# Sums of weight blocks made early and kept in DRAM, and the first products of a two-piece part taken piece by piece

## The chip, the core and the metric

The kernel is one program on one core of a Trainium2 chip. The metric is the device time of one execution in microseconds (us). The core has five engines that each run their own list of instructions in order: TensorE (PE; its weight loads are shown apart as PEld), VectorE (DVE), ScalarE (ACT), GpSimd (POOL) and SyncE (SP, which here only issues DMA transfers). An instruction waits on semaphores for the work of other engines and for transfers; whatever stands behind it on its engine waits with it.

## The reference, cut to what matters

Three stages follow one another: windowed attention, a gated MLP behind an RMS norm, and a second MLP with a softmax-like gate and a layer norm.

```python
x = attention(q, k, v)                      # 4 x 8 heads x 576 x 64; window of 32, or dilated by 4; as rows: 2304 x 512
xn = x / sqrt(mean(x * x) + 1e-06) * rms_g  # 512 wide
g = xn @ w_gate                             # 512 x 1536
y = (g / (1 + exp(-g)) * (xn @ w_val)) @ w_out        # back to 512
h = y @ w_in                                # 512 x 1024
e = exp(h - max(h)); solu = h * e / sum(e)
out = layer_norm(solu) * g_ln @ w_out2      # 2304 x 512
```

## The kernel before, in words

Every fp32 product is taken as three products of split numbers: a tensor is split into a high half (`xh`, `uh`, the first index of `w`), rounded by ACT (L304), and the rest, its low half, subtracted by DVE or POOL (L313). The helper `mm3` issues high by high, high by low and low by high (L890, L891, L892).

The 2304 rows are cut into nine pieces of 256. Parts 0, 2, 3 and 4 are two pieces (512 rows), part 1 is one. The work goes through these stages, by the clock of the profiled run: attention of the first pieces (0 to 32 us); the first MLP on part 0, while its weights come from DRAM and are split (v0 to v2, 32 to 153 us); part 1 (v3, to 219 us); part 2, pieces 3 and 4 (v4, to 344 us); parts 3 and 4 jointly (to 462 us); the second products of those two and the second MLP's weights (to 540 us); the second MLP on all 18 row tiles (to the end). Attention of later pieces (`scores`, L619; softmax on DVE and ACT; `values`, L665) runs between the MLP's matmuls, a few steps ahead of need. Where a piece's attention is done, its rows are normed and split into `xh` and `xl`.

Weights: for each of the twelve blocks f of 128 columns, SP fetches `w_gate`, `w_val` and `w_out` raw (L342; `raw` has five places), ACT and DVE rework the words (L357, L362, L366), ACT rounds the high half, DVE or POOL subtracts the low one. The halves stay in SBUF. For use much later, ACT also issues a copy of the plain words of `w_gate` and `w_val` to DRAM: step `kept`, L392, tile `pw`, 24 transfers of 256 KB.

The joint stage multiplies two parts by a pair of weight blocks with seven block products instead of eight (`m1` to `m7`, L1177), for twelve groups q. Four of the factors are sums and differences of weight blocks. In each group, `sload` (SP, L1140) reads two plain blocks back from `pw` into `sc`, `scomb` (L1145; DVE for q below 3, POOL from 3 on) makes four sums of 128x256, `shigh` (ACT, L304, into `shl`) and `slow` (DVE, L313) split them. Then come the products, with ACT copying partial sums from bank to bank in between (`seed`, L1184). `m7` needs both the split sums and a `seed` that stands behind `shigh` on ACT.

The second MLP makes each pair of row tiles r by seven block products, `p1` to `p7` (L1499 to L1501), from weights that are fetched and split at 468 to 533 us; ACT or DVE copy partial sums between them (`u2`: `ha` to `he`). The four column sums (L1507: `c11`, `c22`, `c21`, `c12`, DVE) read the banks of those products. Then a pair is normed, transposed (`t`, PE), split into `lt` (ACT, then DVE, L313) and multiplied by the last weights (`o`, L1572 to L1574). `y` L1432 are sums of loaded `y` blocks, made by DVE or POOL.

The order of all this is not written out. Each step is handed to a planner (`Plan`) with what it needs, the tiles it takes, the engines that may run it with a cost for each, and a due time. The planner simulates the engines by these costs, takes whichever ready step can start first (among those close together the one due first), and so fixes the engine of each step and the order on each engine. A table of small shifts to due times (`NUDGE`) is the same in both kernels. PE's order from 342 us on is forced by a list, `line`. A change of any cost or due time can thus move instructions anywhere.

Of the kernel before, what the change touches and what calls it, by code (L numbers as in the profile page):

```python
# [256 lines left out]
def tile_attention_glu_solu(ctx: ExitStack, tc: tile.TileContext, qk_d, v_d, w1_d, win2_d, wout2_d,  # L257
# [71 lines left out]
    def prepare(stage, f, cuts, srcs, scales, dues, needs=(), lead=((1, 0), "joined", 0)):  # L329
# [67 lines left out]
        for n, c in enumerate(cuts):  # L397
            w, due = 512 * len(c), dues[c[0]]
            one, two, act, pool_ = 0.15 + w / 1920, 0.15 + w / 960, 0.2 + w / 1200, 0.25 + w / 500
            plan.add((key, "shifted", n), {"a": act}, shifted(c), [(key, "fetch", i) for i in c], due=due)  # L400
            plan.add((key, "parts", n), {"d": one}, parts(c), [(key, "fetch", i) for i in c], due=due)
            plan.add((key, "joined", n), {"d": two}, joined(c), [(key, "parts", n), (key, "shifted", n)] +
                     [lead] * (key != lead[0]) + [(key, "joined", 0)] * (n > 0),
                     takes=([("wf", wf)] if n == 0 else []) + ([("cl", st), ("ch", (st, 1))] if (key, "joined", n) == lead else []),
                     uses=[wf, st, (st, 1)], due=due)
            before = [(key, "joined", n)]
            for i in c:
                if scales[i] is not None:
# [485 lines left out]
    def mlp(v, due):  # L894
# [60 lines left out]

        ready = [[(x, k, t) for t in pieces for x in ("high", "low")] for k in range(2)]
        ys = [("y", p, k) for k in range(KD)]
        for f in fs:
            d = due + 10 * f
            for part, key, shift in ((0, "g", 0), (1, "vp", 3)):  # L960
                for i, ks in enumerate(((0, 1), (2, 3))):
# [4 lines left out]
                    if part == 0 and i == 0 and (f > fs[0] or v in (1, 2)):  # L966
                        before = [("vp", v, f - 1, 1) if f > fs[0] else ("vp", v - 1, HALVES - 1, 1)]
                    plan.add(name, {"t": cost}, into(part, f, (key, v, f), ks),
                             before + [made[1, f, part]] + (ready[i] if f == fs[0] and part == 0 else []),
# [42 lines left out]
    def joint():  # L1012
# [22 lines left out]
        for f in range(STASHED):  # L1035
# [17 lines left out]
            add(("stash", f), {"s": 1.35}, keep_, [made[1, f, 2], ("g", 4, f // 2, 0)], due=150)  # L1053
# [66 lines left out]
        def group_(q):  # L1120
            fp, X = divmod(q, 2)
            fs = (2 * fp, 2 * fp + 1)
            sc, shl, far = ("sc", q), ("shl", q), q > 1 and q % 2 == 0
            tag_of = {"A": "a", "E": "a", "D": "a", "B": "g", "C": "vp"} if q % 2 == 0 else \
# [14 lines left out]
            def load(e):  # L1139
                nc.sync.dma_start(out=scratch().rearrange("p a m -> p (a m)"), in_=plain_w[fp, X].rearrange("p i m -> p (i m)"))  # L1140

            def combos(e):
                t = scratch()
                for out_, a, b, op in ((3, 2, 3, ALU.add), (2, 0, 2, ALU.subtract), (0, 3, 0, ALU.subtract), (1, 1, 0, ALU.subtract)):
                    ENG[e].tensor_tensor(t[:, out_], t[:, a], t[:, b], op)  # L1145

            key_c = [("scl",)] * far
# [141 lines left out]
    def operands(j, needs_of):  # L1289
# [79 lines left out]
    def w_out2():  # L1369

        st = ("stage", 2)
        for g in range(2):
# [8 lines left out]
            for i in range(4):  # L1381
# [16 lines left out]
                plan.add((key, "fetch"), {"s": 1.35}, lambda e, rw=rw, k=k: nc.sync.dma_start(out=words(rw).rearrange("p n t -> p (n t)"),  # L1398
# [194 lines left out]
    def second_stage(stage_1, last):  # L1593
# [73 lines left out]
        def tile_steps(i):  # L1667
# [3 lines left out]
            for q in range(2):  # L1671
# [3 lines left out]
                    takes=[lt] if q == 0 else [], uses=[tp[1], lt[1]], due=due - 60 if r else 5800)  # L1675
                add(("lt", i, q, 1), {"d": 0.7}, lambda e, q=q: p_lt(i, q, 1, e), [("lt", i, q, 0)], uses=[tp[1], lt[1]], due=due - 60 if r else 5800)
# [163 lines left out]
```

## Time and profile before

| | |
|---|---|
| median of 3 runs | 740.66 us (739.85 to 741.54) |
| profiled execution | 737.58 us |
| its span, first to last instruction | 735.8 us |
| PE busy | 715.8 us, 97% |
| DVE, ACT, POOL busy | 66%, 50%, 21% |
| granted TensorE clock, mean | 0.995 |
| moved by DMA | 90.94 MB, 124 GB/s in the mean |

Durations are read from the profiled execution, which lies 3.08 us under the median; 1.78 us of its time lie outside the span. A granted clock of 1.00 is the upper of TensorE's two levels (2.4 GHz). At that level matmuls of 512 columns follow each other every 0.23 us, although the records last 0.39 us, since they overlap.

### The profile page before, as it was taken

Reading aid. Unit: us, or ns where it says so; the run is one execution under the profiler, and the core shown is the slowest. Engines: PE = TensorE matmul, PEld = TensorE weight load, DVE = VectorE, ACT = ScalarE, POOL = GpSimd, SP = SyncE. Lnnn points to the kernel's source line nnn. Section 1 sums busy time; section 2 is a strip of 40 time slices with the busy share of each in tenths; the row PEclk is TensorE's granted clock in tenths of the full one; section 3 lists DMA queues with packets and bytes.
Section 4 is the critical chain, followed back from the end, with each engine's and each line's share of the span. In section 5 each row is a group of like instructions: output and inputs, shape, how many; then the busy total and the mean of one; then the engine's idle time right before and its main releaser. Section 6 shows DMA issues by size and latency. Waiting matters only on the chain.

```text
span 735.8 us, 11918 instructions
## 1 busy us (share of the span) xinstructions
PE 715.8 (97%) x4565; PEld 599.1 (81%) x4565; DVE 485.4 (66%) x933; ACT 368.5 (50%) x810; POOL 155.2 (21%) x181
## 2 busy tenths in 40 slices
PE   7988999999999999999999999999999999999998
PEld 5876878899997788888788888888777888888887
DVE  4876998555556657559777676688767776655552
ACT  2874745444554446334555555264455555444341
POOL 0210035222212122020455110046043110101110
PEclk9999999999999999999999999999999999999999
DMA  9989433232347643102411103784132111000001
GB/s 329 401 313 397 169 123 127 77 138 82 114 137 247 230 145 119 39 21 68 141 57 58 58 0 104 234 292 147 54 115 73 57 44 58 29 15 29 30 29 44
DMA packets 42009, 90.94 MB, mean 124 GB/s; under 512 B 4192, under 2 KB 14432, under 8 KB 41952
## 3 DMA queue, kind: packets, MB, share of 16 engines
q1 hardware_dynamic: 38496, 83.89, 33.1%
q10 hardware_dynamic: 3456, 6.29, 2.3%
q8 instruction: 36, 0.59, 0.3%
q14 instruction: 21, 0.17, 0.1%
HBM read 69.72 MB, written 20.45 MB: 123 GB/s over the span
## 4 chain that ended last, share of the span: by engine, by line
PE 79%; DMA 7%; DVE 4%; POOL 3%; issue 3%; ACT 2%; SPq 1%; ACTq 0%; POOLq 0%; DVEq 0%
PE ca L1177 6%; PE o L1573 4%; PE o L1572 4%; PE o L1574 4%; PE y L890 4%; PE g L890 4%; PE y L892 4%; PE y L891 4%; PE g L891 4%; PE g L892 4%; PE vp L890 4%; PE vp L892 3%; PE vp L891 3%; PE pv L665 3%; DMA raw<-w 3%
## 5 line engine op out<-in xcount | busy, mean ns | idle before, releaser
L1572 PE MATMUL o<-w,lt 128*128 128x512 f32 (+1 forms) x152 | 58.9, 388 | 0.0
L1574 PE MATMUL o<-w,lt 128*128 128x512 f32 (+1 forms) x152 | 57.6, 379 | 0.0
L1573 PE MATMUL o<-w,lt 128*128 128x512 f32 (+1 forms) x152 | 57.5, 379 | 0.0
L313 POOL TENSOR_TENSOR w<-wf,w 128x512 fp32r<-128x512 f32 (+1 forms) x15 | 30.5, 2038 | 122.8 <-ACT w L304 122.8
L890 PE MATMUL y<-uh,w 128*128 128x512 f32 (+1 forms) x148 | 54.1, 366 | 0.0
L892 PE MATMUL y<-uh,w 128*128 128x512 f32 (+1 forms) x148 | 51.8, 350 | 0.0
L891 PE MATMUL y<-uh,w 128*128 128x512 f32 (+1 forms) x148 | 51.7, 349 | 0.0
L632 ACT ACTIVATE s<-s,nm 128x64 f32<-128x64 f32 x120 | 40.2, 338 | 20.6 <-DVE nm L627 18.0
L1145 POOL TENSOR_TENSOR sc<-sc 128x256 f32<-128x256 f32 x36 | 33.5, 931 | 68.5 <-DMA yT<-yo 32.9
L921 ACT ACTIVATE u<-g 128x512 f32<-128x512 f32 (+1 forms) x37 | 19.1, 516 | 54.3 <-PE g L892 54.3
L772 POOL TENSOR_TENSOR sq<-x 128x256 f32<-128x256 f32 x28 | 18.4, 659 | 131.8 <-ACT x L304 71.9
L927 DVE SCALAR_TENSOR_TENSOR u<-u,g 128x512 f32<-128x512 f32 (+1 forms) x37 | 21.6, 584 | 33.0 <-ACT u L921 32.9
L890 PE MATMUL g<-xh,w 128*128 128x512 f32 (+1 forms) x100 | 41.7, 417 | 0.3 <-ACT xh L304 0.3
L1540 POOL TENSOR_SCALAR st<-st 128x1 f32<-128x1 f32 x18 | 7.0, 388 | 160.6 <-ACT sq L1531 160.5
L890 PE MATMUL vp<-xh,w 128*128 128x512 f32 (+1 forms) x100 | 40.1, 401 | 0.0
L891 PE MATMUL g<-xl,w 128*128 128x512 f32 (+1 forms) x100 | 39.4, 394 | 0.2 <-DVE xl L313 0.2
L892 PE MATMUL g<-xh,w 128*128 128x512 f32 (+1 forms) x100 | 39.2, 392 | 0.0
L892 PE MATMUL vp<-xh,w 128*128 128x512 f32 (+1 forms) x100 | 38.3, 383 | 0.0
L891 PE MATMUL vp<-xl,w 128*128 128x512 f32 (+1 forms) x100 | 38.1, 381 | 0.0
L931 DVE SCALAR_TENSOR_TENSOR u<-u,vp 128x512 f32<-128x512 f32 (+1 forms) x37 | 21.7, 585 | 22.7 <-PE vp L892 22.3
L304 ACT CAST w<-wf 128x512 fp32r<-128x512 f32 (+1 forms) x40 | 28.3, 727 | 15.4 <-DVE wf L366 7.5
L304 ACT ACTIVATE pT<-tp,half 128x256 f32<-128x256 f32 x60 | 25.3, 469 | 20.8 <-PE tp L647 20.8
(282 smaller groups left out, 2071.4 us busy)
## 6 DMA issues: line engine op xcount, KB each, us to landing
raw<-w SPq DMA_DIRECT2D x36, 512.0 KB, 7.7
pw<-wf ACTq DMA_DIRECT2D x24, 256.0 KB, 3.2
sc<-pw SPq DMA_DIRECT2D x12, 512.0 KB, 3.3
vt<-v SPq DMA_DIRECT2D x22, 256.0 KB, 3.4
qk<-qk SPq DMA_DIRECT2D x14, 400.0 KB, 4.2
wo<-w SPq DMA_DIRECT2D x9, 512.0 KB, 4.9
wst<-wo SPq DMA_DIRECT2D x9, 512.0 KB, 3.7
yT<-yo SPq DMA_DIRECT2D x16, 256.0 KB, 2.8
```

Source lines behind the costliest of these rows:

```text
L304: nc.scalar.copy(dst, src) if scale is None else nc.scalar.mul(dst, src, scale)
L313: ENG[e].tensor_tensor(dst, a, b, ALU.subtract)
L632: nc.scalar.activation(T[s_][:, i], T[s_][:, i], AF.Exp, bias=st["nm"][:, i:i + 1], accum_out=sm[:, i:i + 1])
L665: nc.tensor.matmul(x[64 * j:64 * j + 64, 64 * i:64 * i + 64], T[vt][:, i, j, :], T[pT][:, i, 64 * j:64 * j + 64], start=True, stop=True)
L890: nc.tensor.matmul(acc, wh, xh, start=first, stop=False)
L891: nc.tensor.matmul(acc, wh, xl, start=False, stop=False)
L892: nc.tensor.matmul(acc, wl, xh, start=False, stop=last)
L1145: ENG[e].tensor_tensor(t[:, out_], t[:, a], t[:, b], op)
L1177: nc.tensor.matmul(acc(x), w, y, start=not more and j == 0 and n == 0, stop=j == 1 and n == 2, skip_group_check=True)
L1572: nc.tensor.matmul(o, lt[:, 0, k], w[:, 0], start=(k == 0), stop=False)
L1573: nc.tensor.matmul(o, lt[:, 0, k], w[:, 1], start=False, stop=False)
L1574: nc.tensor.matmul(o, lt[:, 1, k], w[:, 0], start=False, stop=(k == NF2 - 1))
```

## The change

The four sums of each group q are made long before the joint stage and kept in DRAM (`es`, 512 KB each). For groups below 6 (weight blocks f below 6), `ewhole` adds the two halves of the split weights that lie in SBUF (DVE, two instructions of 128x512 per group), so that the plain copies of these blocks are no longer written: `pw` shrinks from 24 transfers to 12. For groups 6 to 11, `eload` reads the plain blocks back from `pw`. Then `ecomb` (POOL or DVE) makes the four sums, `estore` (SP) writes them. The place in SBUF is that of inputs which part 0 (rooms 0 and 1) and part 1 (room 2) no longer need, so the work can start when `out` of v2 ends, and for the later groups when v3's `vp` ends. In the joint stage `sload` reads the finished sums, and `scomb` is gone.

The products of v4 with its first block of `w_gate` are taken piece by piece: 12 matmuls of 256 columns that need piece 3, then 12 that need piece 4, instead of 12 of 512 columns that need both, six at a time.

The copies of `w_out` blocks to DRAM (`stash`) may start only later in v4. The planner's costs of fetching the second MLP's weights rise (1.35 to 2.0 and 2.6), two due times of `lt` go from 5800 to 5930, and for the pair r = 2 `p4` is taken ahead of `p7`. The last lines of each place, as changed:

```diff
-            if any(i < 2 for i in c):
+            if f >= NF1 // 2 and any(i < 2 for i in c):
...
-    plain_w = {(f, x): dr.tile([P, 2, 512], F32, tag=f"pw{f}_{x}", name=f"pw{f}_{x}") for f in range(NF1 // 2) for x in range(2)}
+    plain_w = {(f, x): dr.tile([P, 2, 512], F32, tag=f"pw{f}_{x}", name=f"pw{f}_{x}") for f in range(NF1 // 4, NF1 // 2) for x in range(2)}
...
+        def by_piece(part, f, key, j):
+            def emit(e):
+                if j == 0:
+                    tag, i = plan.where[key]
+                    T[key] = ps.tile([P, 512], F32, tag=f"{tag}{i}", name=tag)[:, 0:n]
+                w, m = w1[f, part], slice(TP * j, TP * j + TP)
+                for k in range(KD):
+                    c = slice(k * P, (k + 1) * P)
+                    mm3(T[key][:, m], w[:, 0, c], w[:, 1, c], x_of(0, k)[:, m], x_of(1, k)[:, m], k == 0, k == KD - 1)
...
+                    alone = v == 4 and f == 0 and part == 0
+                    plan.add(name, {"t": cost}, by_piece(part, f, (key, v, f), i) if alone else into(part, f, (key, v, f), ks),
+                             before + [made[1, f, part]] + ([(x, k, pieces[i]) for x in ("high", "low") for k in range(2)] if alone else
+                                                            ready[i] if f == fs[0] and part == 0 else []),
...
-            add(("stash", f), {"s": 1.35}, keep_, [made[1, f, 2], ("g", 4, f // 2, 0)], due=150)
+            add(("stash", f), {"s": 1.35}, keep_, [made[1, f, 2], ("g", 4, f + 2, 0)], due=150)
...
-            def load(e):
-                nc.sync.dma_start(out=scratch().rearrange("p a m -> p (a m)"), in_=plain_w[fp, X].rearrange("p i m -> p (i m)"))
...
+            def whole(i):
+                def emit(e):
+                    w = w1[fs[i], X]
+                    ENG[e].tensor_tensor(flat(room()[:, 2 * i:2 * i + 2]), w[:, 0], w[:, 1], ALU.add)
+                return emit
...
+            def plain(e):
+                nc.sync.dma_start(out=flat(room()), in_=plain_w[fp, X].rearrange("p i m -> p (i m)"))
...
             def combos(e):
-                t = scratch()
+                t = room()
                 for out_, a, b, op in ((3, 2, 3, ALU.add), (2, 0, 2, ALU.subtract), (0, 3, 0, ALU.subtract), (1, 1, 0, ALU.subtract)):
                     ENG[e].tensor_tensor(t[:, out_], t[:, a], t[:, b], op)
 
+            def store(e):
+                T["es", q] = dr.tile([P, 4 * 256], F32, tag=f"es{q}", name=f"es{q}")
+                nc.sync.dma_start(out=T["es", q], in_=flat(room()))
+
+            def load(e):
+                nc.sync.dma_start(out=flat(scratch()), in_=T["es", q])
...
+            first = [("eload" if late else "ewhole", NF1 // 2 * late, *([0] * (not late)))] if q % (NF1 // 2) else []
+            if not late:
+                for i in range(2):
+                    add(("ewhole", q, i), {"d": 0.7}, whole(i), [made[1, fs[i], X]] + ([("ewhole", q, 0)] if i else first or [("out", 2, NF1 - 1, 1)]),
+                        takes=([("ec", ec)] + rooms * (q == 0)) * (i == 0), uses=held, due=50 + q)
+                ends = [("ewhole", q, i) for i in range(2)]
+            else:
+                add(("eload", q), {"s": 1.35}, plain, [((1, f), "kept", 0 if f >= SINGLE else X) for f in fs] + (first or [("vp", 3, NF1 - 1, 1)]),
+                    takes=[("ec2", ec)] + rooms * (q == NF1 // 2), uses=held, due=50 + q)
+                ends = [("eload", q)]
+            add(("ecomb", q), {"p": 3.0, "d": 1.6}, combos, ends, uses=held, due=50 + q)
+            add(("estore", q), {"s": 1.35}, store, [("ecomb", q)], uses=held, due=50 + q)
...
-            add(("sload", q), {"s": 1.35}, load, [((1, f), "kept", 0 if f >= SINGLE else X) for f in fs] + [("ox",)] +
-                ([("sload", q - 1 - (q > 2))] if q else []),
+            add(("sload", q), {"s": 1.35}, load, [("estore", q), ("ox",)] + ([("sload", q - 1 - (q > 2))] if q else []),
...
-            add(("scomb", q), {"d": 1.6} if q < 3 else {"p": 3.0}, combos, [("sload", q)], uses=[sc] + key_c, due=due)
-            add(("shigh", q), {"a": 1.15}, lambda e: put(e, s_split()[:, 0], scratch()), [("scomb", q)],
+            add(("shigh", q), {"a": 1.15}, lambda e: put(e, s_split()[:, 0], scratch()), [("sload", q)],
...
-            plan.add((key, "fetch", x), {"s": 1.35}, fetch(x), [("rwopen",)], takes=[("raw", ("raw", key, x))],
+            plan.add((key, "fetch", x), {"s": 2.0}, fetch(x), [("rwopen",)], takes=[("raw", ("raw", key, x))],
...
-                plan.add((key, "fetch"), {"s": 1.35}, lambda e, rw=rw, k=k: nc.sync.dma_start(out=words(rw).rearrange("p n t -> p (n t)"),
+                plan.add((key, "fetch"), {"s": 2.6}, lambda e, rw=rw, k=k: nc.sync.dma_start(out=words(rw).rearrange("p n t -> p (n t)"),
...
-                add(("lt", i, q, 1), {"d": 0.7}, lambda e, q=q: p_lt(i, q, 1, e), [("lt", i, q, 0)], uses=[tp[1], lt[1]], due=due - 60 if r else 5800)
+                    takes=[lt] if q == 0 else [], uses=[tp[1], lt[1]], due=due - 60 if r else 5930)
+                add(("lt", i, q, 1), {"d": 0.7}, lambda e, q=q: p_lt(i, q, 1, e), [("lt", i, q, 0)], uses=[tp[1], lt[1]], due=due - 60 if r else 5930)
...
-                h(r, "p1", "p5", "p6") * (q == 0) + h(r, "p2", "p7", "p4")
+                (h(r, "p1", "p5", "p6", "p2", "p4", "p7") if q == 0 else h(r, "p2", "p7", "p4"))
```

What the planner makes of it is seen in the order of each engine. On ACT, at 43 to 47 us, stand the splits of the weight block f = 1 (`w`, one tile for each of its three matrices) and the copies to `pw`; before:

```order
L921 ACTIVATE u<-g 128x256
L304 CAST w_0_642<-wf 128x512
L392 DMA pw_0_96<-wf 128x512
L304 CAST w_1_657<-wf 128x512
L392 DMA pw_1_97<-wf 128x512
L357 ACTIVATE raw_2_513<-raw_2_513 128x512
L357 ACTIVATE raw_0_528<-raw_0_528 128x512
L304 CAST uh<-u 128x256
```

and in the changed kernel:

```order
L304 CAST w_0_623<-wf 128x512
L921 ACTIVATE u<-g 128x256
L304 CAST w_1_639<-wf 128x512
L357 ACTIVATE raw_2_507<-raw_2_507 128x512
L357 ACTIVATE raw_0_521<-raw_0_521 128x512
L357 ACTIVATE raw_1_544<-raw_1_544 128x512
```

The two transfers to `pw` are gone there, and the ACT work closes up.

On POOL, from the end of the joint stage to 510 us, stand the sums of the joint stage (`sc`), then splits and sums of the second MLP's weights (`w`, `wf`) and of loaded blocks (`y`); before:

```order
L1145 TENSOR_TENSOR sc<-sc 128x256 x36
L313 TENSOR_TENSOR w_0_404<-wf,w_0_404 128x512
L313 TENSOR_TENSOR wf<-wf 128x512
L313 TENSOR_TENSOR w_0_806<-wf,w_0_806 128x512
L313 TENSOR_TENSOR w_0_883<-wf,w_0_883 128x512
L313 TENSOR_TENSOR wf<-wf 128x512 x2
L313 TENSOR_TENSOR w_0_979<-wf,w_0_979 128x512
L1432 TENSOR_TENSOR y<-y 128x256 x4
L313 TENSOR_TENSOR w_0_725<-wf,w_0_725 128x512
L313 TENSOR_TENSOR w_1_494<-wf,w_1_494 128x512
L313 TENSOR_TENSOR wf<-wf 128x512 x3
```

and in the changed kernel:

```order
L797 TENSOR_TENSOR r<-r,mhalf 128x2
L313 TENSOR_TENSOR w_0_623<-wf,w_0_623 128x512
L313 TENSOR_TENSOR wf<-wf 128x512 x3
L313 TENSOR_TENSOR w_0_1241<-wf,w_0_1241 128x512
L313 TENSOR_TENSOR wf<-wf 128x512
L1481 TENSOR_TENSOR y<-y 128x256 x4
```

The 36 sums are gone. Of twelve weight steps six are left: eight went to DVE, two came from it. The sums of `y` (now L1481) stand at the end.

On DVE, at 547 to 553 us, stand the column sums of the pair r = 1 (`h`, by the custom instruction shown as ISA) and the low halves `lt` of its first row tile; before:

```order
L313 TENSOR_TENSOR lt<-tp,lt 128x512 x2
L1507 ISA h,st<-e,hb 128x512
L1507 ISA st 128x1
L1507 ISA h,st<-e,hd,st 128x512
L1507 ISA st 128x1
L1507 ISA h,st<-h,hb,st 128x512
L1507 ISA st 128x1
```

and in the changed kernel (L1507 is now L1556):

```order
L1556 ISA h,st<-e,hb 128x512
L1556 ISA st 128x1
L1556 ISA h,st<-e,hd,st 128x512
L1556 ISA st 128x1
L1556 ISA h,st<-h,hb,st 128x512
L1556 ISA st 128x1
L313 TENSOR_TENSOR lt<-tp,lt 128x512 x2
```

`lt` has moved from ahead of the three column sums to behind them. The last of the three reads the bank `hb` of `p3`.

## Rows read from the trace of the kernel before

**Rows 1.** Windows: us, PE, PEld, DVE, ACT, POOL busy, PE clock, DMA share, GB/s

```profile
65.00:70.00 5.00, 5.00 (x23) 3.99 (x19) 1.06 (x2) 0.20 (x1) 0.00 (x0) 0.66 1.03 410
...
80.00:153.00 73.00, 73.00 (x437) 59.24 (x435) 55.61 (x83) 38.31 (x96) 25.02 (x15) 1.00 0.26 91
...
153.00:219.00 66.00, 66.00 (x744) 64.02 (x743) 35.18 (x100) 33.34 (x125) 13.79 (x18) 1.00 0.39 127
...
219.00:262.00 43.00, 42.50 (x379) 33.62 (x378) 27.09 (x65) 21.67 (x82) 9.24 (x13) 1.00 0.67 235
```

**Rows 2.** What PE waited for: us in total, times, longest

```profile
PE sp L619 <- DMA qk<-qk: 3.6, 2, 2.1
...
PE ha L1499 <- ACT he L304: 2.0, 2, 1.5
...
PE ca L1177 <- ACT cb L1184: 1.8, 1, 1.8
...
PE hb L1499 <- DVE st L1507: 0.8, 1, 0.8
...
PE g L890 <- ACT xh L304: 0.3, 1, 0.3
...
PE g L891 <- DVE xl L313: 0.2, 1, 0.2
```

**Rows 3.** Timeline of PE, 59.5 to 69 us: start, busy, line, idle before

```profile
62.33 0.69 PE L619 MATMUL sp<-qk 128*64 128x64 f32 x16 [2.13 <-DMA qk<-qk]
...
64.52 0.69 PE L619 MATMUL sp<-qk 128*64 128x64 f32 x16 [1.50 <-DMA qk<-qk]
...
65.13 0.80 PE L890 MATMUL g<-xh,w 128*128 128x512 f32 x1
...
68.63 0.39 PE L892 MATMUL g<-xh,w 128*128 128x512 f32 x1
```

**Rows 4.** Chain of waits, 40 to 70 us: start, us, what

```profile
44.14 8.72 DMA pw<-wf
...
55.97 8.50 DMA qk<-qk
```

**Rows 5.** What SP waited for over the run: us in total, times, longest

```profile
SPq L342 <- DMA pw<-wf: 23.1, 6, 6.8
```

**Rows 6.** Timeline of PE, last products of v3, 256 columns

```profile
218.06 0.28 PE L892 MATMUL y<-uh,w 128*128 128x256 f32 x1
...
218.18 0.28 PE L890 MATMUL y<-uh,w 128*128 128x256 f32 x1
```

**Rows 7.** The joint stage's sums (ns min/median/max), and ACT behind them

```profile
L1145 POOL TENSOR_TENSOR sc<-sc x36: 734/743/1599, 357.3 to 425.5; 128x256 f32<-128x256 f32 x36
...
L1145 DVE TENSOR_TENSOR sc<-sc x12: 419/424/426, 338.2 to 354.4; 128x256 f32<-128x256 f32 x12
...
362.24 1.04 ACT L304 CAST shl<-sc 128x1024 fp32r<-128x1024 f32 x1 [2.28 <-POOL sc L1145]
```

**Rows 8.** Timeline, 497 to 522 us: POOL's sums of y, ACT before u2

```profile
497.67 4.10 POOL L1432 TENSOR_TENSOR y<-y 128x256 f32<-128x256 f32 x4
...
521.37 0.72 ACT L304 ACTIVATE w<-wf,gln 128x512 fp32r<-128x512 f32 x1 [1.43 <-DVE wf L1395]
```

**Rows 9.** Timeline, 547 to 552 us: lt, p3, the column sum, o

```profile
547.96 1.29 DVE L313 TENSOR_TENSOR lt<-tp,lt 128x512 fp32r<-128x512 f32 x2 [1.21 <-ACT lt L304]
...
549.90 0.50 PE L1499 MATMUL hb<-w,w 128*128 128x512 f32 x1 [0.84 <-DVE st L1507]
...
551.40 0.39 PE L1572 MATMUL o<-w,lt 128*128 128x512 f32 x1
...
551.60 0.75 DVE L1507 CUSTOM_DVE_ANT_0 h<-h,hb,st 128x512 f32<-128x512 f32 x1 [0.85 <-PE hb L1501]
```

**Rows 10.** Timeline, 486.8 to 489.2 us, POOL and DVE

```profile
486.97 3.16 POOL L313 TENSOR_TENSOR w<-wf,w 128x512 fp32r<-128x512 f32 x2 [1.13 <-ACT w L304]
...
487.18 1.78 DVE L1321 SCALAR_TENSOR_TENSOR wf<-raw 128x512 uint32<-128x512 uint32 x1
```

More of the change, by code (lines that the diff above doesn't have):

```diff
@@ L967, in mlp @@
                         before = [("vp", v, f - 1, 1) if f > fs[0] else ("vp", v - 1, HALVES - 1, 1)]
-                    plan.add(name, {"t": cost}, into(part, f, (key, v, f), ks),
-                             before + [made[1, f, part]] + (ready[i] if f == fs[0] and part == 0 else []),
+                    alone = v == 4 and f == 0 and part == 0
+                    plan.add(name, {"t": cost}, by_piece(part, f, (key, v, f), i) if alone else into(part, f, (key, v, f), ks),
+                             before + [made[1, f, part]] + ([(x, k, pieces[i]) for x in ("high", "low") for k in range(2)] if alone else
+                                                            ready[i] if f == fs[0] and part == 0 else []),
                              takes=[(key, (key, v, f))] if i == 0 else [],
@@ L1123, in group_ @@
             sc, shl, far = ("sc", q), ("shl", q), q > 1 and q % 2 == 0
+            late = fp >= NF1 // 4
             tag_of = {"A": "a", "E": "a", "D": "a", "B": "g", "C": "vp"} if q % 2 == 0 else \
@@ L1137, in s_split, with room @@
                 return T[shl]
-            def load(e):
-                nc.sync.dma_start(out=scratch().rearrange("p a m -> p (a m)"), in_=plain_w[fp, X].rearrange("p i m -> p (i m)"))
+            def room():
+                i, half_ = divmod(plan.where["ec", q][1], 2)
+                i += 2 * late
+                if ("room", i) not in T:
+                    T["room", i] = xn.tile([P, 2, 4, 256], F32, tag=("bh0", "bl0", "ch0")[i], name="ec")
+                return T["room", i][:, half_]
@@ L1142, in combos, with flat @@
+            def flat(t):
+                return t.rearrange("p a m -> p (a m)")
+            def whole(i):
+                def emit(e):
+                    w = w1[fs[i], X]
+                    ENG[e].tensor_tensor(flat(room()[:, 2 * i:2 * i + 2]), w[:, 0], w[:, 1], ALU.add)
+                return emit
+            def plain(e):
+                nc.sync.dma_start(out=flat(room()), in_=plain_w[fp, X].rearrange("p i m -> p (i m)"))
             def combos(e):
-                t = scratch()
+                t = room()
@@ L1144, in combos @@
                 for out_, a, b, op in ((3, 2, 3, ALU.add), (2, 0, 2, ALU.subtract), (0, 3, 0, ALU.subtract), (1, 1, 0, ALU.subtract)):
                     ENG[e].tensor_tensor(t[:, out_], t[:, a], t[:, b], op)
+            def store(e):
[3 more added lines that the diff above has]
+                nc.sync.dma_start(out=flat(scratch()), in_=T["es", q])
+            rooms, ec = [("ch", ("rooms", 2))] if late else [("bh", ("rooms", 0)), ("bl", ("rooms", 1))], ("ec", q)
@@ new lines, in group_ @@
+            held = [k for _, k in rooms] + [ec]
+            first = [("eload" if late else "ewhole", NF1 // 2 * late, *([0] * (not late)))] if q % (NF1 // 2) else []
[8 more added lines that the diff above has]
+                ends = [("eload", q)]
@@ L1674, in tile_steps @@
                 add(("lt", i, q, 0), {"a": 0.59}, lambda e, q=q: p_lt(i, q, 0, e), [("t", i, q), ("switch",)] + ([("lt", i, 0, 0)] if q else []),
-                    takes=[lt] if q == 0 else [], uses=[tp[1], lt[1]], due=due - 60 if r else 5800)
-                add(("lt", i, q, 1), {"d": 0.7}, lambda e, q=q: p_lt(i, q, 1, e), [("lt", i, q, 0)], uses=[tp[1], lt[1]], due=due - 60 if r else 5800)
+                    takes=[lt] if q == 0 else [], uses=[tp[1], lt[1]], due=due - 60 if r else 5930)
+                add(("lt", i, q, 1), {"d": 0.7}, lambda e, q=q: p_lt(i, q, 1, e), [("lt", i, q, 0)], uses=[tp[1], lt[1]], due=due - 60 if r else 5930)
             for a, n in ([(0, DM)] if i != SEQ[-1] else [(0, DM // 2), (DM // 2, DM // 2)]):
```

2 rows, old and new, of the table plan are left out of this document.

## The prediction

> **What bounds the kernel now.** The page's busy shares come first: PE is busy 715.8 of 735.8 us, all others far less. So only what stops PE, or slows its clock, can move the time. Next comes the list of what PE waited for. Leaving out waits ahead of 42 us, up to where PE's order is the same in both kernels, six entries remain [rows 2]: 3.6 us for `qk`, 2.0 for ACT's `he` (two waits, the longer 1.5, so the other 0.5), 1.8 for ACT's `cb`, 0.8 for DVE's `st`, and 0.3 and 0.2 for the first products of the two-piece part. That is 8.7 us. Third, the timeline of PE behind the longest wait: two stops ahead of the scores [rows 3], then nine starts from 65.13 to 68.63, 3.50 us for eight steps. At full rate they take 1.36 for six, as `p3` does without its restart (1.50 less 0.11) [rows 9], so 1.8 for eight; 1.7 us are lost to the clock, granted 0.66 in the mean of this stretch [rows 1]: starts 0.43 apart are the lower level, 1.2 GHz. The reader is to see that PE had been idle for most of the 5 us before it fell. Last, the chain of waits names what made `qk` late [rows 4].
>
> **The change, part by part.**
>
> *Early copies dropped.* The chain reads: a copy to `pw`, under way from 44.14, takes 8.72 us to land; SP stands until then; only behind its fetches comes the load of `qk`, issued at 55.97 and landed after 8.50 [rows 4]. SP's fetches waited 23.1 us in six waits for such copies [rows 5], though the fetches don't read them: the program lets its transfers take turns on eight completion semaphores, and the next user of one waits for the last. The changed kernel writes only the later 12 of the 24 copies, so none is left ahead of these loads. Besides the wait, twelve times 256 KB, 3.1 MB, leave the transfers of the first 100 us; at 410 GB/s, the rate of 65 to 70 us [rows 1], that is 7.7 us of bandwidth, about half of it ahead of `qk`. To be harmless the last load must land 64.52 - 60.2 = 4.3 us earlier (PE's first stop began 2.13 ahead of 62.33, [rows 3]). The blocked stretch alone, 44.14 to 52.86, is longer; I estimate 6 to 8 us. The two stops (3.6) go, and with them what the clock cost (1.7): -5.3. From below nothing is gained if other fetches hold SP as long.
> What is late next is weights: PE then wants each block 5.3 us sooner. From 80 to 153 us DVE is busy 55.6 of 73 us [rows 1], so there are 17 us to give, and in 65 to 70 us it did only 1.1 us of work, for lack of data, which now arrives sooner. I count nothing back, and keep 0 to 5.3 for the range.
>
> *First products by piece.* 24 matmuls of 256 columns for 12 of 512: at 0.12 us apart [rows 6] 2.9 us, against 2.7 (twice the six of `p3`), so +0.2. Piece 3 is the one whose attention ended a piece earlier, so neither the 0.3 nor the 0.2 us [rows 2] is waited for at the start. Piece 4 is wanted 1.4 us of products and at least 0.7 us of scores (one block, [rows 3]) later. Net -0.3.
>
> *Sums kept in DRAM.* ACT's `shl` of q = 3 waited 2.28 us for POOL's four sums [rows 7], `cb` stood behind it, and PE behind that 1.8 us. In the changed kernel `shl` waits only for a load; `sload` 3 stands on SP ahead of the stores of `y`, its place free once `slow` 1 is done, before the groups' need. -1.8. The sums themselves move to 153 to 262 us: 12 adds of halves by DVE at 0.65, as `lt` of that size [rows 9] (7.8 us), seven groups of four sums by DVE at 0.42 [rows 7] (11.8), five by POOL at 0.74 to 1.60 [rows 7] (15 to 32). DVE is idle there for 31 us in v3 and 16 in v4's first half [rows 1], so its 20 us are covered; PE depends on DVE in chains (`silu`, `prod`, `uhigh`, `ulow`), but takes `ulow` one block later, and no new work stands longer than 3 us in a row. DMA gains 18 transfers of 512 KB in stretches that use 0.39 and 0.67 of it [rows 1]. 0, with 0 to 3 us for a load held up, below.
>
> One thing speaks against that cover. While POOL made two splits of 3.16 us together, a DVE instruction of 128x512 took 1.78 [rows 10]; `lt` of that size takes 0.65 [rows 9]. The Trainium skill, "SBUF — State Buffer", section "Who interferes with whom", says that a DVE instruction with two inputs in SBUF and a GpSimd one that reads SBUF exclude each other, the later one blocked to the end of the other. These rows agree: 1.78 is about the rest of POOL's first split, 1.4, and 0.65. By the rule a split of piece 4, on DVE while POOL makes the sums of q = 6, would take up to 1.6 us longer each; by the lead of 2.1 us just counted PE then waits about 1 us there, 732.7 in all; without it, not at all. This is inside the range.
>
> *Second MLP.* Three waits are touched.
> (a) `he` for `p7` of r = 0, 1.5 us. ACT's copy stood behind the rounding of a weight, which began at 521.37 when DVE had joined it [rows 8]; DVE had begun with these output weights only when POOL's chain ended, and in it stand 4.10 us of `y` sums [rows 8]. On POOL six of twelve weight steps are left, and the sums stand last. DVE takes on six net (6 x 0.65 = 3.9 us), but loses a neighbour that doubled its times [rows 10]. I follow DVE's order and get these weights some 4 us sooner; 1.5 suffice. -1.5.
> (b) `he` for `p7` of r = 2, 0.5 us: `p4`, six matmuls or 1.36 us, now comes first. -0.5.
> (c) `st`, 0.8 us: `p3` waited for a column sum that stood behind two `lt` (547.96, 1.29) [rows 9]. With `lt` behind all column sums that wait goes. But the last column sum reads `p3`'s bank, and `o` needs `lt`. From the rows: the sum began 1.70 us after `p3` (549.90 to 551.60) and lasted 0.75, one `lt` is 0.65, so `o` can start 3.1 us after `p3`; `p3` takes 1.50 [rows 9]. A new wait of 1.6 us stands in place of 0.8: +0.8.
> Sum of the part: -1.2.
>
> *Restarts.* The first matmul behind a wait lasted 0.50 instead of 0.39 [rows 9]; four such fewer (`g`, `ca`, two of `ha`; `o` restarts in place of `hb`): -0.4.
>
> **The sum.** -5.3 - 0.3 - 1.8 - 1.2 - 0.4 = -9.0. From the profiled 737.58 (span 735.8 and 1.8 around it) that gives 728.6; the median lies 3.08 higher, and 740.66 - 9.0 = 731.7. I predict 731.7 us.
>
> **Rivals.**
> *1. Weights become the bound.* With `qk` on time PE runs into weight splits between 62 and 130 us. For: DVE was busy 55.6 of 73 us there, in an order fixed ahead [rows 1]. Against: idle time in all of it, earlier data. Price: the 5.3 return, in a different place; 731.7 + 5.3 = 737.0.
> *2. SP is blocked by its new stores (slower).* SP is in order. Each of the 12 stores waits for its four sums, and every later load of `qk` and `v` with it. Place: 150 to 262 us, store 3 behind POOL ahead of the load for scores (4,3), then stores 6 to 11, where a reload also waits until a store has landed. With sums of 0.734 the store waits 2.9 us, with 1.60 [rows 7] 6.4 us, and the load is 1 to 2 us late. Each late load costs PE a stop as in rows 3, 1.5 to 2.1, and the clock again, 1.7: about 3.5. Three late loads use up the gain; with four the time is 731.7 + 14 = 745.7. Against: following SP's order I find a load past its need at one place only, and in v4 the scores stand several blocks behind their loads.
> *3. The joint stage keeps its wait.* If `sload` 3 comes late (its place in `sc` is still shared), ACT's `shl` waits for DMA instead of POOL. 731.7 + 1.8 = 733.5.
> *4. The new wait (c) isn't there,* because DVE gets to `lt` sooner than I read from its order: 731.7 - 1.6 = 730.1.
>
> **How the numbers follow.** The forecast with its own spread (728.5 to 734.5, rivals 3 and 4 inside it) has 0.72. Rival 1, in part or whole, has 0.15. Rival 2 has 0.13, of which 0.03 is one late load (still faster) and 0.01 two of them. What a measurement of this kernel can tell from no change is about 0.2%, 1.5 us. Rival 1 is still 4 us faster, unless a smaller loss comes on top (0.05 to no change). So faster has 0.72 + 0.10 + 0.03 = 0.85, no change 0.06, slower 0.09. The range takes in rival 1: 728 to 737.5.
>
> **What would show it.** Right: no wait of PE for `qk` between 59 and 70 us, clock 1.00 there; no `pw` issued by ACT ahead of 80 us; no wait for `cb` near 353 us; none for `he` in the second MLP; a wait of about 1.6 us of `o` for `lt` near 542 us, and none for `st`. Wrong: PE waiting for `w` in 60 to 130 us (rival 1), for `qk` in 150 to 262 us with SP's loads behind `es` stores (rival 2), or for `lt` nowhere.

## The result, and the profile after

The changed kernel takes 730.39 us in the median of six runs (729.41 to 734.15), the kernel before 740.36 beside it (738.58 to 742.35): a ratio of 0.987 (95%: 0.984 to 0.990). Predicted were 731.7 us, in 728.0 to 737.5. The profiled execution took 730.41 us with a span of 728.6, against 737.58 and 735.8 before: 7.2 us less, where the medians fell by 10. The profiled execution of before lay 2.8 us below its median, that of after at it.

What PE waited for in the changed kernel from 42 us on (us in total, times, longest), the whole list:

```profile
PE o L1623 <- DVE lt L313: 1.0, 1, 1.0
PE ha L1548 <- ACT he L304: 0.6, 1, 0.6
PE tp L647 <- DVE x L308: 0.3, 1, 0.3
PE y L891 <- DVE uh L313: 0.3, 1, 0.3
PE tp L647 <- DVE s L640: 0.2, 1, 0.2
```

Against [rows 2] the entries for `qk`, `ca`, `hb` and both for `g` are gone, and `he` stands at 0.6 us in one wait instead of 2.0 in two. New are 1.0 us of `o` for `lt`, which the prediction names, and three for `x`, `uh` and `s`, 0.8 us together, which it does not.

The windows of 60 to 70, 153 to 219, 219 to 262 and 344 to 462 us (columns as in [rows 1]):

```profile
60.00:70.00 10.00, 10.00 (x72) 8.14 (x71) 9.01 (x17) 4.27 (x6) 0.00 (x0) 1.00 0.67 246
...
153.00:219.00 66.00, 66.00 (x724) 64.29 (x723) 47.55 (x122) 32.29 (x120) 22.64 (x30) 1.00 0.52 176
219.00:262.00 43.00, 42.16 (x377) 33.06 (x376) 30.54 (x73) 21.92 (x87) 16.81 (x24) 1.00 0.82 277
...
344.00:462.00 118.00, 118.00 (x522) 97.64 (x522) 78.33 (x113) 63.74 (x105) 0.00 (x0) 1.00 0.23 76
```

From 60 to 70 us PE runs through at a clock of 1.00. From 153 to 262 us DVE does the sums: 47.55 + 30.54 against 35.18 + 27.09 busy, 15.8 us more; and from 219 to 262 PE now stands for 0.84 us. In the joint stage POOL is empty and PE full.

What SP waited for ([rows 5] for before). The first line is the fetches of weights; they now wait only for the landing of earlier fetches. The second is the reloads, which wait for stores:

```profile
SPq L342 <- DMA raw<-w: 17.3, 19, 1.0
...
SPq L1170 <- DMA es<-ec: 9.7, 4, 3.1
```

No fetch of weights waits for a copy any more: the 23.1 us for `pw` are gone. SP issues the two loads of `qk` that were late at 43.94 and 46.51 us; before, 54.72 and 55.97. They take 10.1 to 11.0 us to land, since the transfers are full there, so the second is in place by 57.5 at the latest, 7 us earlier than the 64.47 of before; PE takes up its scores at 61.6.

### The profile page after: what moved, and what is told of

The parts are those of the page before. It is cut to its first block, busy times and chain, and to the rows that moved or that the text cites. A ratio compares the mean times of both kernels' runs of the same rounds, so it can differ in the third digit from the quotient of the medians.

```text
span 728.6 us, 11970 instructions
## 1 busy us (share of the span) xinstructions
PE 715.4 (98%) x4577; PEld 599.3 (82%) x4577; DVE 498.2 (68%) x965; ACT 367.7 (50%) x810; POOL 126.3 (17%) x161
## 4 chain that ended last, share of the span: by engine, by line
PE 89%; DMA 6%; DVE 3%; POOL 1%; ACT 1%; issue 0%; SPq 0%; DVEq 0%; ACTq 0%; POOLq 0%
PE ca L1226 7%; PE y L890 7%; PE y L892 6%; PE y L891 6%; PE o L1623 5%; PE o L1622 4%; PE o L1621 4%; PE vp L890 4%; PE g L890 4%; PE vp L892 3%; PE g L892 3%; PE vp L891 3%; PE g L891 3%; PE cd L1226 2%; PE cb L1226 2%; PE cc L1226 2%
## 5 line engine op out<-in xcount | busy, mean ns | idle before, releaser
L313 POOL TENSOR_TENSOR w<-wf,w 128x512 fp32r<-128x512 f32 (+1 forms) x13 | 22.6, 1744 | 211.4 <-ACT w L304 211.4
L1622 PE MATMUL o<-w,lt 128*128 128x512 f32 (+1 forms) x152 | 57.5, 378 | 0.0
L632 ACT ACTIVATE s<-s,nm 128x64 f32<-128x64 f32 x120 | 40.2, 339 | 14.5 <-DVE nm L627 10.1
L304 ACT CAST uh<-u 128x512 fp32r<-128x512 f32 (+1 forms) x37 | 19.9, 537 | 28.8 <-DVE u L931 27.7
```

Of the source, the lines that this page charges most:

```text
L304: nc.scalar.copy(dst, src) if scale is None else nc.scalar.mul(dst, src, scale)
L313: ENG[e].tensor_tensor(dst, a, b, ALU.subtract)
L632: nc.scalar.activation(T[s_][:, i], T[s_][:, i], AF.Exp, bias=st["nm"][:, i:i + 1], accum_out=sm[:, i:i + 1])
L1622: nc.tensor.matmul(o, lt[:, 0, k], w[:, 1], start=False, stop=False)
```

## The experiments

Ratios are to the kernel before on the same chip, whose median was 739.9 (first four), 739.2 (next four) and 739.5 us (last three). Three chips were used, so kernels of different groups are compared by ratio only. The diffs show the line that matters; `...` stands for lines left out.

**The early copies issued again** (the changed kernel with all 24 copies).

```
-            if f >= NF1 // 2 and any(i < 2 for i in c):
+            if any(i < 2 for i in c):
...
```

> The changed kernel, and the twelve early copies of weight blocks to DRAM (f below 6, 256 KB each) are issued again by ACT where they stood, though nobody reads them. My theory: they are what made qk late. PE waits again for qk near 55 to 65 us, 3 to 4 us in two stops, with a stretch at the lower clock behind them: 4 to 6 us slower than the changed kernel, 735 to 736. Rival: qk came late because of the order of SP's fetches, which the change altered; then no wait for qk and under 1 us slower.

Measured: 736.84 us, ratio 0.9955 (0.9935 to 0.9975). PE's timeline from 60 to 69 us and the mean of 66 to 69:

```profile
63.28 0.69 PE L619 MATMUL sp<-qk 128*64 128x64 f32 x16 [1.95 <-DMA qk<-qk]
65.49 0.84 PE L619 MATMUL sp<-qk 128*64 128x64 f32 x16 [1.53 <-DMA qk<-qk]
```
```profile
66.00:69.00 3.00, 3.00 (x14) 2.31 (x12) 1.00 (x2) 0.00 (x0) 0.00 (x0) 0.50 1.01 386
```

Both stops are back, and behind them the clock falls to 0.50, its lower level. SP again waits 24.2 us for copies and issues `qk` at 56.33. What this costs is read between two products of PE that all kernels have, the first `y` and the `g` product that stands at 68.63 us before [rows 3]. Before, the changed kernel, and the copies issued again:

```profile
44.14 0.28 PE L890 MATMUL y<-uh,w 128*128 128x256 f32 x1
```
```profile
45.58 0.28 PE L890 MATMUL y<-uh,w 128*128 128x256 f32 x1
...
64.58 0.39 PE L892 MATMUL g<-xh,w 128*128 128x512 f32 x1
```
```profile
45.28 0.28 PE L890 MATMUL y<-uh,w 128*128 128x256 f32 x1
...
69.59 0.40 PE L892 MATMUL g<-xh,w 128*128 128x512 f32 x1
```

That is 24.49, 19.00 and 24.31 us: the copies account for 5.3 of the 5.5 us gained there. The medians lie 6.4 us apart, more than the forecast 4 to 6. In the profiled execution PE also stands 2.1 us for `uh` near 238 us, with the clock falling behind it: the reload told of below, whose delay is larger here than in the changed kernel.

**The same copies with a sixteenth of their bytes** (32 of 512 columns stored; nothing reads them).

```
-                        nc.scalar.dma_start(out=plain_w[f // 2, i][:, f % 2], in_=wf_((i,))[:, 0])
+                        n_ = 512 if f >= NF1 // 2 else 32
+                        nc.scalar.dma_start(out=plain_w[f // 2, i][:, f % 2, 0:n_], in_=wf_((i,))[:, 0, 0:n_])
...
```

> As copies_back, with the same twelve early transfers, but each of 32 of the 512 columns (16 KB instead of 256 KB). Two theories of how a copy delays qk. By the share of completion semaphores alone, a small copy that queues behind the fetches lands nearly as late as a large one and still holds SP: 2 to 5 us slower than the changed kernel. By bytes (3.1 MB at 400 GB/s, 7.7 us of all transfers), the wait is gone: within 1 us of the changed kernel.

Measured: 734.12 us (729.81 to 736.59), ratio 0.9916 (0.9885 to 0.9947). By the time alone, 3.7 us slower than the changed kernel, the first theory would seem right. The profile answers better, since most of the loss lies elsewhere: PE stands 1.7 us for `uh` and 2.1 us for `s` between 230 and 250 us, at the reload told of below. SP's and PE's waits:

```profile
SPq L342 <- DMA pw<-wf: 19.6, 5, 7.0
```
```profile
PE sp L620 <- DMA qk<-qk: 0.9, 1, 0.9
```

SP still stands 19.6 us for copies and issues the two loads of `qk` at 55.35 and 56.30 us, about 1 us earlier than with the whole copies and no earlier than the kernel before; they land in 6.0 us instead of 7.4. PE waits 0.9 instead of 3.8 us and the clock stays at 1.00 from 60 to 69 us. The stretch between the two products:

```profile
44.91 0.28 PE L891 MATMUL y<-uh,w 128*128 128x256 f32 x1
...
65.30 0.40 PE L893 MATMUL g<-xh,w 128*128 128x512 f32 x1
```

It takes 20.39 us. So with SP standing as before, taking the bytes away gives back 3.9 of the 5.3 us, about three quarters. The converse, SP not standing while the bytes are moved, was not run. It need not cost the remaining quarter only: the two causes act on one wait, and the changed kernel, where SP doesn't stand for copies, issues the loads some 10 us earlier.

**First products of the part not by piece.**

```
-                    alone = v == 4 and f == 0 and part == 0
+                    alone = False
```

> The changed kernel, with the first products of the two-piece part made again as 12 matmuls of 512 columns that need both pieces. By my sum 0.3 us slower (0.5 of waits for xh and xl come back, 0.2 us of extra starts go). Rival: PE had caught up with the splits of piece 4, since every stage before is shorter, so that the wait is longer than before, 1 to 2 us slower.

Measured: 734.29 us, ratio 0.9923 (0.9894 to 0.9952). The 0.27 and 0.23 us for `xh` and `xl` are back, no longer than before, so the rival fell. But a new wait of 1.7 us of `ms` for `x`, between the starts at 238.54 and 240.61, stands beside them, with the lower clock behind it: with these products in another order, the reload's delay falls elsewhere. So the time can't price the products by piece, but the trace can. From the last `y` of v3 to the first `vp` of v4 PE does the same work in these kernels. Before and the changed kernel:

```profile
219.14 0.28 PE L892 MATMUL y<-uh,w 128*128 128x256 f32 x1
219.69 0.49 PE L890 MATMUL g<-xh,w 128*128 128x512 f32 x1 [0.27 <-ACT xh L304]
220.41 0.50 PE L891 MATMUL g<-xl,w 128*128 128x512 f32 x1 [0.23 <-DVE xl L313]
...
225.53 0.50 PE L890 MATMUL vp<-xh,w 128*128 128x512 f32 x1
```
```profile
214.83 0.28 PE L892 MATMUL y<-uh,w 128*128 128x256 f32 x1
214.95 0.28 PE L890 MATMUL g<-xh,w 128*128 128x256 f32 x1
...
220.27 0.50 PE L890 MATMUL vp<-xh,w 128*128 128x512 f32 x1
```

That is 6.39 and 5.44 us; without the products by piece it is 6.37 again (213.01 to 219.38). They bring 0.9 us.

**The second MLP's edits undone** (costs of the fetches, place of `lt`, the line of `p7` and `p4`).

```
...
-                (h(r, "p1", "p5", "p6", "p2", "p4", "p7") if q == 0 else h(r, "p2", "p7", "p4"))
+                h(r, "p1", "p5", "p6") * (q == 0) + h(r, "p2", "p7", "p4")
```

> The changed kernel, with the second MLP's edits undone: fetch costs 1.35, the two due times of lt 5800, p7 ahead of p4 for r = 2. By my theory the wait of p7 of r = 2 for ACT comes back (0.5 and restart), p3 waits 0.8 for its column sum again, and o does not wait for lt (1.0 less); p7 of r = 0 waits as long as POOL's chain makes it, 0.6 to 1.5. In all 0 to 1.5 us slower. Rival: with the joint stage's sums gone from POOL these edits are worth nothing, within 0.3 us.

Measured: 731.09 us, ratio 0.9886 (0.9855 to 0.9916), against 0.9869 for the changed kernel: 0 to 1 us. PE's waits here:

```profile
PE ha L1548 <- ACT he L304: 1.8, 2, 1.4
...
PE hb L1548 <- DVE st L1556: 0.8, 1, 0.8
```

By the two lists, 1.8 + 0.8 make room for 0.6 + 1.0: the three edits bring 1.0 us, where 1.2 were predicted.

**The kernel before, with the joint stage's sums on DVE alone.**

```
-            add(("scomb", q), {"d": 1.6} if q < 3 else {"p": 3.0}, combos, [("sload", q)], uses=[sc] + key_c, due=due)
+            add(("scomb", q), {"d": 1.6}, combos, [("sload", q)], uses=[sc] + key_c, due=due)
```

> The kernel before, with one word changed: the four sums of the joint stage are made by DVE for every group, not by POOL from q = 3 on; nothing is made early or kept in DRAM. My theory of that stage's wait (1.8 us of PE for cb): POOL's four sums of 4.9 us are too slow, so DVE's 1.6 to 1.8 us take it away, 1.8 to 2.1 us faster than before, and the early sums are not needed for this gain. Rival: the reload comes so late that any sum in that place keeps PE waiting; then within 0.5 us of before. The wait for qk near 60 us stays as in before by both.

Measured: 737.85 us, ratio 0.9985 (0.9966 to 1.0004). The joint stage, 344 to 462 us:

```profile
344.00:462.00 118.00, 118.00 (x523) 97.69 (x522) 96.46 (x158) 65.13 (x107) 0.00 (x0) 1.00 0.23 76
```

PE stands nowhere in it, and DVE has 21 us to spare. From its first to its last product the stage takes 116.73 us, against 118.79 before and 116.77 in the changed kernel. So the 1.8 us wait was one of POOL's speed, and neither sums made early nor a second pass through DRAM were needed to take it away. The time falls by 1.3 us where 1.8 to 2.1 were expected; the interval still holds 0.3 us to the slower side, so the gain is shown by the trace and not by the time.

**The sums of groups 6 to 11 on POOL alone**, to free DVE from the wait for the reload.

```
-            add(("ecomb", q), {"p": 3.0, "d": 1.6}, combos, ends, uses=held, due=50 + q)
+            add(("ecomb", q), {"p": 3.0} if late else {"p": 3.0, "d": 1.6}, combos, ends, uses=held, due=50 + q)
```

> The changed kernel, with the sums of groups 6 to 11 on POOL alone. In the changed kernel DVE stood 3.5 us at 224 to 227 us for the reload of plain weights (ec from pw), and PE then waited 0.28, 0.33 and 0.24 us in 229 to 242 us; in copies_back and copies_small, where the transfers ran otherwise, 2.1 us, with the clock falling behind it. My theory: DVE's wait for the reload is the cause, so these waits vanish, 1 us faster than the changed kernel and less scattered. Rival, by the shared port: POOL's sums make DVE's instructions beside them longer, up to 1.8 us, and PE waits as long or longer: same or 1 us slower.

Measured: 736.06 us, ratio 0.9957 (0.9939 to 0.9974): this theory fell. PE's longest wait, and POOL at that time:

```profile
PE ms L787 <- POOL sq L778: 5.2, 1, 5.2
```
```profile
228.03 3.51 POOL L1175 TENSOR_TENSOR ec<-ec 128x256 f32<-128x256 f32 x4 [3.39 <-DMA ec<-pw]
233.55 2.41 POOL L1175 TENSOR_TENSOR ec<-ec 128x256 f32<-128x256 f32 x3 [2.02 <-DMA ec<-pw]
```

The waits for `uh` and `x` went, but POOL is in order too: it stood 3.39 and 2.02 us for two reloads, and the squares of the attention's norm stood behind the sums. Behind PE's stop the clock is at 0.50 from 238 to 244.5 us. A queue that stands moves its cost to whatever is behind it.

**The low half `lt` ahead of the second half's column sums.**

```
+        plan.steps["lt", 1, 0, 1]["needs"].append(("c22", 1))
+        plan.steps["c12", 1]["needs"].append(("lt", 1, 1, 1))
```

> The changed kernel, with DVE's lt of the first row tile bound to stand behind the column sum c22 and ahead of c12. By my theory o no longer waits for lt (1.0 us and a restart gone) and p3 still doesn't wait: 1.1 us faster than the changed kernel. Rival: c21 or a later sum then comes late and the wait moves on, within 0.3 us.

Measured: 728.12 us (727.38 to 729.63), ratio 0.9845 (0.9821 to 0.9869). The wait of `o` is gone and none takes its place. In the two profiles the products behind `o` gain 1.0 us on those ahead of it, as expected. Beside the changed kernel's ratios, 0.9869 and 0.9884, the time is 1.8 to 2.9 us less; the intervals overlap, and 1.3 of the 2.0 us between the profiles lie in the start-up.

**The last two together, and ACT's copy `he` ahead of a block's high half**, one line more:

```
+        plan.steps["yhigh", 1, 0]["needs"].append(("u2", 0))
```

> late_pool and lt_fix together, and ACT's copy u2 of r = 0 set ahead of the rounding of the next y block, for the 0.6 us that PE still waits for he at 515 us. By addition 2.5 to 3 us faster than the changed kernel, 727 to 728. If POOL's sums disturb DVE, only the last two count: 1.5 to 1.9 us.

Measured: 734.33 us, ratio 0.9924 (0.9903 to 0.9945). PE's wait for POOL is there again (4.9 us, ahead of 239.62). The wait for `he` went, and `hb` waits 0.7 us for `st` in its place: nothing to gain there.

**The sums of groups 8 to 11 bound behind the attention output that comes late enough**, so that nobody comes to them before the reload has landed.

```
-            add(("ecomb", q), {"p": 3.0, "d": 1.6}, combos, ends, uses=held, due=50 + q)
+            add(("ecomb", q), {"p": 3.0, "d": 1.6}, combos, ends + [("out", 4, q - 8, 1)] * (q >= 8), uses=held, due=50 + q)
```

> The sums of groups 8 to 11 now may start only behind the attention output out(4, q-8, 1), so neither VectorE nor GpSimd comes to a sum whose piece is still being stored and loaded again. Theory (VectorE standing 3.5 us for the reload costs TensorE its waits at 230.8, 232.5 and 242.1, 0.28 + 0.33 + 0.24 us with their restarts): these waits leave TensorE's list, the time is about 1 us below the changed kernel's (some 729.4 us where that has 730.4) and scatters less. Rival (the wait only moves): another wait of TensorE of about the same size stands between 225 and 345 us, and the time is within 0.4 us of the changed kernel's.

**The same, with `lt` earlier**: this line and the two added above for `lt`.

> The spaced sums together with the low half's copy lt(1,0,1) ahead of the sums of the second half, which took the 1.0 us wait of o. Theory: the two are at different places and add: about 1 us below the kernel with the earlier copy alone, 727 to 728 us here, 2 to 2.5 us below the changed kernel. Rival: the same as the earlier copy alone (within 0.4 us of it, about 728.3 us), if the reload's waits were not on the path that sets the end.

**The changed kernel again**, beside these two, unedited.

> The changed kernel again, beside the two others on the same chip. Theory: 730.4 us, ratio to the kernel before 0.985 to 0.989, with the 2 to 3 us waits for q and k gone and about 1 us for the reload and 1.0 us for the low half in TensorE's list again. Rival (the waits at the reload were chance of one run): TensorE's waits for the evictions uh and x at 230 to 243 us are under 0.3 us together this time.

Measured: 729.82 us (ratio 0.9860, 0.9832 to 0.9889), 728.43 (0.9846, 0.9815 to 0.9877), and 731.59 (0.9884, 0.9858 to 0.9910) for the changed kernel. What it lost to the reload this time, DVE first, then PE:

```profile
227.93 1.87 DVE L1175 TENSOR_TENSOR ec<-ec 128x256 f32<-128x256 f32 x4 [4.59 <-DMA ec<-pw]
```
```profile
231.21 0.50 PE L891 MATMUL y<-uh,w 128*128 128x512 f32 x1 [1.39 <-DVE uh L313]
...
232.94 0.44 PE L647 MATMUL tp<-ident,s 128*128 128x128 f32 x2 [0.30 <-DVE x L308]
```
```profile
233.00:235.00 2.00, 2.00 (x7) 1.61 (x8) 1.75 (x4) 1.78 (x8) 1.76 (x2) 0.56 1.00 386
235.00:236.60 1.60, 1.60 (x17) 0.95 (x17) 1.42 (x4) 0.58 (x4) 0.00 (x0) 0.50 0.19 74
```

DVE stood 4.59 us, PE 1.39 + 0.30, and then the granted clock was at 0.56 and 0.50 up to 236.6 us. The rival, that the reload's waits were chance of one run, fell: they are larger here. With the sums bound later, PE waits nowhere between 219 and 262:

```profile
219.00:262.00 43.00, 43.00 (x356) 34.60 (x355) 30.15 (x72) 19.77 (x75) 11.06 (x16) 1.00 0.77 260
```

The gain of 1.8 us beside the changed kernel is more than the 1 us expected, in intervals that overlap. With `lt` earlier as well it is 3.2 us. The ratio of this last kernel is that of the earlier `lt` alone (0.9846 and 0.9845), measured on another chip: whether the two add beyond that kernel is open. Both are the fastest seen, 1.5% below before. The two kernels with the sums bound later have a wait that the changed kernel has not, 0.41 us of `ca` for `cc` in the joint stage; whether the later sums bring it was not followed up.

## Why the prediction was right, and where its steps were off

*Early copies.* Right in size: between the two products named above the changed kernel gains 5.5 us in the two profiles; predicted were 5.3. Rival 1 did not come about: no wait for a weight, DVE 9.01 of 10 us busy at 60 to 70, so the work blocked before was done at once. That the copies are the cause is shown by issuing them again. How SP's standing, which the prediction named first, and the bytes share it is open in part: with the standing left in, the bytes make three quarters. Rows 4 could not tell them apart, since the standing and the load on the transfers come together there.

*By piece: right in kind, too small.* The two waits are gone, as predicted, and the products follow on from the part before without a stop. They bring 0.9 us, where 0.3 and a restart of 0.1 were predicted. The term mis-sized is the price of the two stops: it took their idle times, 0.27 + 0.23. From start to start they took 0.55 and 0.72 us (lines above), where 0.12 [rows 6] and 0.23 are usual, so 0.9 us were lost.

*Sums in DRAM: the 0 us for their making was wrong.* The wait in the joint stage is gone, with its restart: the stage takes 2.0 us less, predicted 1.8 + 0.1. The step that failed is "no new work stands longer than 3 us in a row". It counted DVE's work and left out its wait:

```profile
227.49 1.88 DVE L1175 TENSOR_TENSOR ec<-ec 128x256 f32<-128x256 f32 x4 [3.48 <-DMA ec<-pw]
```

The reload of group 8 may start only when its place in `ec` is free, that is when an earlier group's sums have been stored; it was issued at 222.31 us and took about 5, with DMA 0.82 busy in that window. DVE reached the sums at 224.0, stood 3.48 us, and the splits that PE wanted stood behind it: in this execution 0.28 + 0.33 + 0.24 us. What it cost PE in all is read from that first `vp` of v4 to the first product of the joint stage, in the profile of each kernel that has the same work between them:

| kernel | us |
|---|---|
| before; before with the joint sums on DVE | 118.68; 118.64 |
| changed; changed again | 119.94; 122.11 |
| `lt` earlier; second MLP's edits undone | 120.03; 120.68 |
| copies again; small copies; not by piece | 122.83; 124.65; 123.38 |
| sums bound later; the same with `lt` earlier | 118.71; 118.71 |

With the sums bound later the time is that of before: the sums themselves cost nothing, as predicted. What costs is the standing for the reload, 1.3 to 6.0 us in the seven other executions with these sums, the clock behind it included. In each of the seven DVE stands for it, between 2.4 and 5.3 us at its longest. Rival 2 had the chain of store and reload, but looked for its victim on SP. The range had 0 to 3 us for a load held up, so the case lay inside it.

*DVE beside POOL.* The splits of piece 4 did become slower beside POOL's sums:

```profile
215.35 2.25 DVE L313 TENSOR_TENSOR xl<-x,xh 128x512 fp32r<-128x512 f32 x2 [0.27 <-ACT xh L304]
```
```profile
215.18 3.83 POOL L1175 TENSOR_TENSOR ec<-ec 128x256 f32<-128x256 f32 x4 [5.93 <-PE y L892]
```

Two splits took 2.25 us instead of 1.29 [rows 9], four sums 3.83 instead of 4 x 0.734 = 2.94 [rows 7]: each lost about 0.9 us to the other. The Trainium skill, "SBUF — State Buffer", section "Who interferes with whom", has the two exclude each other; these rows agree in kind. But both splits together lost 1.0, where the prediction took up to 1.6 each, and PE did not wait for them. The prediction's own check was loose as well: 1.4 and 0.65 make 2.05, where the row had 1.78.

*Second MLP.* (a) 0.9 us came of 1.5 and a restart. The working expected the last weights some 4 us sooner, with POOL's sums of `y` standing last and so out of the way. They were not out of the way: they ran at 505 us, beside DVE's splits of just these weights.

```profile
505.36 4.18 POOL L1481 TENSOR_TENSOR y<-y 128x256 f32<-128x256 f32 x4 [4.24 <-DMA y<-yT]
```
```profile
504.42 0.69 DVE L1444 SCALAR_TENSOR_TENSOR wf<-raw 128x512 uint32<-128x512 uint32 x1
...
507.72 1.22 DVE L1444 SCALAR_TENSOR_TENSOR wf<-raw 128x512 uint32<-128x512 uint32 x1
```

Four instructions of DVE, from 505.69 to the next start at 509.86, took 4.2 us beside the sums; the same kinds take 2.2 just before. ACT then waited for DVE, and its copy stood behind that rounding and one more, as before:

```profile
514.46 0.72 ACT L304 ACTIVATE w<-wf,gln 128x512 fp32r<-128x512 f32 x1 [0.47 <-DVE wf L1444]
515.09 0.82 ACT L304 CAST w<-y 128x768 fp32r<-128x768 f32 x1
515.81 0.57 ACT L304 COPY he<-ha 128x512 f32<-128x512 f32 x1
```

That these 2 us are what keeps 0.6 us of the wait is argued, no run shows it. (b) as predicted, no wait at `p7` of r = 2. (c) The wait is of the kind predicted, 1.0 instead of 1.6 us:

```profile
543.85 0.39 PE L1622 MATMUL o<-w,lt 128*128 128x512 f32 x1
545.24 0.50 PE L1623 MATMUL o<-w,lt 128*128 128x512 f32 x1 [1.00 <-DVE lt L313]
```
```profile
543.83 0.75 DVE L1556 CUSTOM_DVE_ANT_0 h<-h,hb,st 128x512 f32<-128x512 f32 x1 [0.61 <-PE hb L1550]
...
544.50 1.28 DVE L313 TENSOR_TENSOR lt<-tp,lt 128x512 fp32r<-128x512 f32 x2
```

The chain of column sum and `lt` is the predicted one. Only the third of `o`'s three products reads the low half; the first two start without it and cover the rest. Rival 4 (no wait) did not come about, rival 3 neither.

*The sum.* Read at the same products in the two profiles, the changed kernel lies +1.4 us behind before at the first `y`. From there it makes -5.5 (to the `g` product), -0.3 (to the end of v3), -0.9 (to the first `vp` of v4, by piece), +1.3 (to the joint stage, the reload), -2.0 (joint stage), -0.9 (to `p7` of r = 0) and -0.4 (to the last product; (b), (c), restarts): -7.3, of which the span keeps 7.2. Predicted were -9.0. By piece gave 0.5 us more than counted, the reload took 1.3 that were not counted. (A slip of the working, 1.36 for 1.50 less 0.11, moves nothing.)

The 1.4 us are no part of the change. They come from a stretch at 39 to 43 us, the changed kernel first, then before:

```profile
39.00:41.00 2.00, 1.95 (x10) 1.35 (x10) 1.90 (x5) 1.99 (x4) 0.00 (x0) 0.50 1.04 414
41.00:43.00 2.00, 2.00 (x15) 1.52 (x14) 0.40 (x1) 0.17 (x1) 1.27 (x1) 0.71 1.02 406
```
```profile
39.00:41.00 2.00, 1.91 (x18) 1.69 (x18) 1.90 (x6) 1.89 (x4) 0.00 (x0) 1.00 0.93 358
```

PE had stood for most of 36 to 39 us in both (0.85 and 0.69 us busy), and only one of them then ran at the lower clock. In the second profile of the changed kernel it is 1.00 from 39 to 43.

The time came out 1.3 us below the forecast although the profile fell 1.8 short, because the medians of before and after lie further apart than their profiles. The granted clocks point to a reason: 0.995 in the mean of the profiled execution of before, but 0.992 over the 49 executions of before beside the experiments, and 0.003 of 737 us are 2.2 us; the changed kernel has 0.996 over its twelve. Those executions were not traced. That the median hit the forecast this closely is thus partly luck.

## What to carry to other kernels

A copy that nobody waits for isn't free while the transfers are full: with the copies a load landed in 7.4 us, with a sixteenth of their bytes in 6.0, and through shared completion semaphores SP stood 19.6 us for them even when they were small. When work is moved into idle time, ask of it not only how long it runs but what it waits for: on an in-order engine its wait is paid by what is queued behind it, and moving the work to another in-order engine moves the bill. With DVE standing 3.48 us PE stood 0.85; with POOL standing 3.39 and 2.02 it stood 5.2. Placing the work later in the same queue, behind an event that comes after the load, took the bill away: 118.71 us for the stretch, as before. And price a short stop of PE from start to start: its idle time alone was half of it here.

## What the runs showed of the hardware

The clock turns small waits into larger ones, and not always: a stop of 1.39 us of PE, and 0.30 shortly after, were followed by a granted clock of 0.56 and 0.50 from 233 to 236.6 us in one execution of the changed kernel; after stops of 0.28 and 0.33 in another it stayed at 1.00. It doesn't by itself explain how a kernel's times scatter by 4 us and more: the changed kernel's runs of 730.41 and 734.15 us have the same mean clock, 0.995, and with small copies 729.81 and 736.59 us both have 0.997. What made the longer ones longer was not traced.
